# Complex mixing by three real products, and an inverse on half the rows of the array

## The chip, the cores and the metric

One core of one Trainium2 chip runs the kernel. The metric is the device time of one execution in microseconds (us), as the median of several runs. Three engines matter here besides the DMA queues: PE (TensorE, matrix products), DVE (VectorE) and ACT (ScalarE); POOL (GpSimd) and SP (SyncE) mainly issue DMAs. Each works through its own instructions in order and waits where an operand isn't there. Products write to PSUM, in eight banks; DVE and ACT read them out.

## The reference

```python
def _attn_ref(x, w_r, w_i, b_r, b_i):            # x: 2 x 3008 x 256
    X = np.fft.rfft(x, axis=1)
    Xr, Xi = X.real, X.imag
    Yr = Xr @ w_r - Xi @ w_i + b_r
    Yi = Xr @ w_i + Xi @ w_r + b_i
    Yr = np.sign(Yr) * np.maximum(np.abs(Yr) - 0.01, 0.0)
    Yi = np.sign(Yi) * np.maximum(np.abs(Yi) - 0.01, 0.0)
    return np.fft.irfft(Yr + 1j * Yi, n=3008, axis=1)

def _moe_ref(x, w_in, w_out):                    # 256 -> 2048 -> 256, on 6016 tokens
    h = x @ w_in
    return (h * np.clip(h + 3.0, 0.0, 6.0) / 6.0) @ w_out

def _moe2_ref(x, w_gate, w_val, w_out):          # 256 -> 1536 -> 256
    g = x @ w_gate
    return (g / (1.0 + np.exp(-g)) * (x @ w_val)) @ w_out
```

The output is the second of these on the first on the transform with its mixing. All is float32.

## The kernel before

The Fourier part is a transform in two stages (47 by 64) with tables, for two batches (`b`). The first stage (`pre`) writes through DRAM (`Bd`). Its 24 groups of frequencies are taken four at a time, so there are twelve **passes** `(b, Q)`, listed in `ORDER`. A pass has four kinds of work:

- `s2(b, Q, dh)`: the second stage, for either half `dh` of the 256 channels: four float32 products from `z` and the table `m` into one PSUM bank, which is then split into a rounded part `hi` and a remainder `lo` (float32r, tile `X`). Of the imaginary columns negated copies are kept too (`nhi`, `nlo`), so that a slice of 128 columns is either (re, im) or (-im, re).
- `ln(b, Q, h)`: the mixing with the weights, for two of the four groups (a "mixing half"). For each group, 12 products of 256 columns: two halves of the channels, two weights, and three products each for the split (`hi` by `wl`, `hi` by `wh`, `lo` by `wh`). The result has real parts on 64 rows and imaginary ones on the other 64. DVE then adds the bias (`yb`), clips to plus or minus 0.01 (`yc`) and subtracts (`yp`): that is the soft threshold.
- `ia(b, Q, h)`: the first stage of the inverse, two float32 products over 128 rows from `yp` and the table `n` (an "inverse half"); ACT copies them to `cs`, and the second half sends `cs` to DRAM (`Cd`).
- `conv1.step()`: a step of converting the first expert's weights, stored as 64-bit words, to float32r pairs, on ACT and DVE; `st` is loaded on SP.

The order of all this is written out by hand in `seq`. For pass p it is: first mixing half of p, first inverse half of p-1, the second stage of p+1 (two halves), second mixing half of p, second inverse half of p-1. From pass 8 on (`FROM`), four `unit()` calls of the first expert stand in between: a unit makes six products of 512 columns into `ph` for one block of 128 hidden features, gates the result (`r`: Relu on ACT, then a product with it on DVE), splits the tile of the unit before it (`lower`: rounded part on ACT, remainder on DVE), and makes six products of 512 columns of the unit two before into the accumulators. `later` holds an instruction back to the start of the next entry of `seq`. PSUM banks go round: eight until pass 7, then five (`few`), with three left to the accumulators.

After pass 7 `post` makes the first block of tokens from `Cd` (tile `ct`, by `inverse`). After the Fourier part the rest of the units run with preparations for the second scheme of the first expert (`plan`); there `fetch(0)` and `fetch(1)` load the first two weight slots, in units 11 and 13. All loads and most stores are issued on SP, in program order; the stores to `Cd` on POOL. The mixing weights are split by POOL in `split_lin`, ahead of the first pass.

Of the kernel before, what the change touches and what calls it, by code (L numbers as in the profile page):

```python
# [42 lines left out]
def dft_tables():  # L43
# [14 lines left out]
    for g in range(NG):  # L58
# [5 lines left out]
        for q in range(2):  # L64
# [3 lines left out]
            fwd2[g, q, 0, :, 0], fwd2[g, q, 0, :, 1] = c, -sn * sg  # L68
            inv1[g, 0, :, q, 0], inv1[g, 1, :, q, 0] = (w * c).T, -(w * sn * sg).T
            if g:  # L70
                fwd2[g, q, 1, :, 0], fwd2[g, q, 1, :, 1] = sn, c * sg
                inv1[g, 0, :, q, 1], inv1[g, 1, :, q, 1] = (w * sn).T, (w * ci * sg).T
    fwd2 = fwd2.reshape(NG, 128, 128).transpose(1, 0, 2).reshape(128, NG * 128)
    inv1 = inv1.reshape(NG, 128, 128).transpose(1, 0, 2).reshape(128, NG * 128)
# [9 lines left out]
def fourier_moe_kernel(ctx: ExitStack, tc: tile.TileContext, x, lin, bias, w1, w2, fwd1, inv2, fwd2,  # L84
# [52 lines left out]
    three = misc.tile([128, 64], F32, name="three")[:, :1]  # L137
    nc.vector.memset(three, 3.0)
    zeros = misc.tile([128, 512], F32, name="zeros")
# [79 lines left out]
    linh = ap_.tile([128, 2, 2, DIM], F32R, name="linh")  # L219
    linl = ap_.tile([128, 2, 2, DIM], F32R, name="linl")  # L220
    bias_sb = ap_.tile([128, DIM], F32, name="bias_sb")
# [37 lines left out]
    def prepare():  # L259
        lin_st = ap_.tile([128, 2, 2, DIM], F32, tag="z", name="lin_st", bufs=3)  # L260
        nc.gpsimd.dma_start(lin_st, lin)
        nc.gpsimd.dma_start(bias_sb, bias)
        for h in range(2):
            nc.gpsimd.memset(room[5][:, h * TC : (h + 1) * TC], 0.0)
        load_x(5)
        m_t[0] = table("m", fwd2, 0, "m0", 6)
        lins.append(lin_st)

    lins = []

    def split_lin():
        lin_st = lins[0]
        for dh in range(2):
            for k in range(2):
                hi, lo, st = linh[:, dh, k], linl[:, dh, k], lin_st[:, dh, k]
                nc.gpsimd.tensor_copy(hi, st)
                nc.gpsimd.tensor_tensor(out=lo, in0=st, in1=hi.bitcast(F32), op=ALU.subtract)
# [4 lines left out]
    def pre(n):  # L282
# [26 lines left out]
        if n in REFILL:  # L309
            load_x(REFILL[n])  # L310

# [22 lines left out]
    m_t, z_t, n_t, X, yp, cs = {}, {}, {}, {}, {}, {}  # L334
# [5 lines left out]

    def load_q(b, Q):
        if (b, Q) in z_t or Q >= NQ:
            return
        if Q not in m_t:
            m_t[Q] = table("m", fwd2, Q, f"m{Q}", 6)
# [6 lines left out]
    def s2(b, Q, dh):  # L352

        if dh == 0:
            t = ap_.tile([128, 2, 2, 4, 3 * K2], F32R, tag="X", name=f"X{b}_{Q}", bufs=2)
            X[b, Q] = [t[:, k] for k in range(2)]
        p = psf[0]([128, 4, 128], f"p2_{b}_{Q}_{dh}")
        for g in range(4):
            nc.tensor.matmul(p[:, g, :], z_t[b, Q][:, g, dh * 128 : (dh + 1) * 128], m_t[Q][:, g, :],
                             start=True, stop=True)  # L360
        hi, lo = (t[:, dh, :, K2:] for t in X[b, Q])
        nhi, nlo = (t[:, dh, :, :K2] for t in X[b, Q])
# [5 lines left out]
    later = []  # L368

    def run(f):  # L370
# [4 lines left out]
        f()  # L375

    def ln(b, Q, h):

        if Q not in n_t:
            n_t[Q] = table("n", inv1, Q, f"n{Q}", 6)  # L380
# [3 lines left out]
        xh, xl = X[b, Q]  # L384
        for i in range(2):
            g = 2 * h + i
            n = 0
            for dh in range(2):
                for k, at in ((0, K2), (1, 0)):
                    sl = (slice(None), dh, g, slice(at, at + 128))  # L390
                    wh, wl = linh[:, dh, k], linl[:, dh, k]
                    nc.tensor.matmul(p[:, i, :], xh[sl], wl, start=n == 0, stop=False)  # L392
                    nc.tensor.matmul(p[:, i, :], xh[sl], wh, start=False, stop=False)
                    nc.tensor.matmul(p[:, i, :], xl[sl], wh, start=False, stop=n == 3)  # L394
                    n += 1
# [751 lines left out]
```

## Time and profile before

| | us |
|---|---|
| runs | 1210.8, 1211.8, 1212.4; median 1211.8 |
| the profiled execution | 1209.68 |
| its span, first to last instruction | 1207.7 |
| PE busy | 1199.2 (99%) |
| DVE busy | 910.1 (75%) |
| ACT busy | 755.2 (63%) |
| Fourier part with its first 16 units, us of the span | 29 to 197 |

A busy share is the union of an engine's records. A product's record is longer than its place in the stream, since the next one starts while it runs out; so PE's pace is read from start to start. The granted clock of TensorE is 1.00 throughout.

### The profile page before, as it was taken

What the parts mean: (1) busy time and instruction counts of PE and PEld (TensorE: products, weight loads), DVE (VectorE), ACT (ScalarE), POOL (GpSimd) and SP (SyncE); (2) the same over time, 40 slices, a digit from 0 to 9 for tenths busy, and PEclk for the clock granted to TensorE, in tenths of its full rate; (3) what the DMA queues carried; (4) which work ended last, traced back from release to release, by engine and by line L of the source; (5) the groups of instructions that cost most, each with busy time, mean ns of one, the idle gap of its engine ahead of it and who ended that gap; (6) DMA issues with size and microseconds to landing.
All of it is one profiled execution on the core that took longest, in us unless ns stands there. A gap on an engine that the chain in (4) does not pass through costs nothing.

```text
span 1207.7 us, 16257 instructions
## 1 busy us (share of the span) xinstructions
PE 1199.2 (99%) x5794; PEld 1009.3 (84%) x5794; DVE 910.1 (75%) x1599; ACT 755.2 (63%) x1379; POOL 52.8 (4%) x81
## 2 busy tenths in 40 slices
PE   9999999999999999999999999999999999999998
PEld 3899888878888888888889888888888888888997
DVE  4577896798988988989988766766766766766665
ACT  2455565677777777777777555665665655655554
POOL 4000003500000000000000000000000000000000
PEclk9999999999999999999999999999999999999999
DMA  8966343764463554554453444644644644644551
GB/s 300 304 240 198 104 130 114 263 221 165 137 239 126 179 182 157 176 188 143 179 195 132 150 159 161 231 164 159 229 162 160 230 157 157 222 157 157 195 193 70
DMA packets 56720, 216.96 MB, mean 180 GB/s; under 512 B 5776, under 2 KB 17392, under 8 KB 44912
## 3 DMA queue, kind: packets, MB, share of 16 engines
q1 hardware_dynamic: 54000, 206.78, 48.6%
q0 software_dynamic: 2496, 9.05, 2.0%
q8 instruction: 45, 0.74, 0.2%
q14 instruction: 35, 0.29, 0.1%
q10 hardware_dynamic: 144, 0.11, 0.0%
HBM read 169.51 MB, written 46.40 MB: 179 GB/s over the span
## 4 chain that ended last, share of the span: by engine, by line
PE 93%; DVE 3%; DMA 2%; ACT 2%; issue 1%; SPq 0%; ACTq 0%; DVEq 0%
PE acc L125 12%; PE acc L127 12%; PE acc L126 11%; PE P L849 8%; PE P L851 8%; PE P L850 8%; PE Tb L849 4%; PE Tb L851 4%; PE Tb L850 4%; PE p L489 3%; PE Q L849 2%; PE Q L851 2%; PE Q L850 2%; PE p L297 2%; PE p L394 2%; PE p L392 2%
## 5 line engine op out<-in xcount | busy, mean ns | idle before, releaser
L905 ACT COPY hold<-P 128x512 f32<-128x512 f32 (+1 forms) x224 | 128.3, 573 | 78.0 <-PE P L851 77.9
L130 DVE TENSOR_TENSOR gated<-s,gated 128x512 fp32r<-128x512 f32 (+1 forms) x144 | 97.4, 676 | 49.8 <-ACT gated L1034 49.7
L527 ACT CAST gated<-r 128x512 fp32r<-128x512 f32 (+1 forms) x160 | 98.0, 613 | 54.8 <-DVE r L896 54.7
L900 DVE TENSOR_TENSOR hold<-Q,hold 128x512 f32<-128x512 f32 (+1 forms) x112 | 75.9, 678 | 64.9 <-PE Q L851 53.5
L125 PE MATMUL acc<-gated,w_o 128*128 128x512 f32 (+1 forms) x320 | 124.5, 389 | 0.0
L130 DVE TENSOR_TENSOR gated<-r,gated 128x512 fp32r<-128x512 f32 (+1 forms) x160 | 107.8, 674 | 21.9 <-ACT gated L527 18.2
L127 PE MATMUL acc<-gated,w_o 128*128 128x512 f32 (+1 forms) x320 | 123.2, 385 | 0.0
L126 PE MATMUL acc<-gated,w_o 128*128 128x512 f32 (+1 forms) x320 | 123.2, 385 | 0.0
L892 ACT ACTIVATE r<-hold,three 128x512 f32<-128x512 f32 (+1 forms) x120 | 85.7, 714 | 40.7 <-DVE hold L900 40.1
L127 PE MATMUL acc<-gated,slot 128*128 128x512 f32 (+1 forms) x288 | 111.1, 386 | 0.0
L125 PE MATMUL acc<-gated,slot 128*128 128x512 f32 (+1 forms) x288 | 111.0, 385 | 0.0
L126 PE MATMUL acc<-gated,slot 128*128 128x512 f32 (+1 forms) x288 | 110.9, 385 | 0.0
L900 DVE TENSOR_TENSOR hold<-P,hold 128x512 f32<-128x512 f32 (+1 forms) x112 | 75.8, 677 | 38.9 <-PE P L851 38.9
L1074 ACT ACTIVATE s<-hold 128x512 f32<-128x512 f32 (+1 forms) x72 | 44.9, 623 | 86.3 <-DVE hold L900 86.3
L900 DVE TENSOR_TENSOR hold<-Tb,hold 128x512 f32<-128x512 f32 (+1 forms) x112 | 76.0, 678 | 27.1 <-PE Tb L851 20.6
L849 PE MATMUL P<-xo,slot 128*128 128x512 f32 (+1 forms) x240 | 92.2, 384 | 2.5 <-DVE hold L900 1.2
L851 PE MATMUL P<-xo,slot 128*128 128x512 f32 (+1 forms) x240 | 91.6, 382 | 0.0
L896 DVE SCALAR_TENSOR_TENSOR r<-r,hold 128x512 f32<-128x512 f32 (+1 forms) x120 | 81.2, 677 | 13.7 <-ACT r L892 12.8
L850 PE MATMUL P<-xo,slot 128*128 128x512 f32 (+1 forms) x240 | 91.5, 381 | 0.0
L1034 ACT CAST gated<-s 128x512 fp32r<-128x512 f32 (+1 forms) x144 | 88.1, 612 | 1.9 <-DVE s L1089 1.9
L1079 ACT ACTIVATE s<-hold 128x512 f32<-128x512 f32 (+1 forms) x72 | 45.0, 625 | 50.4 <-DVE hold L900 50.4
L127 PEld LDWEIGHTS acc<-gated,w_o 128*128 128x128 f32 x320 | 60.1, 188 | 11.3
(174 smaller groups left out, 2919.8 us busy)
## 6 DMA issues: line engine op xcount, KB each, us to landing
slot<-Wd SPq DMA_DIRECT2D x72, 1152.0 KB, 5.1
slot<-Sd SPq DMA_DIRECT2D x40, 896.0 KB, 4.7
st<-in_w SPq DMA_DIRECT2D x68, 256.0 KB, 4.2
Wd<-slot SPq DMA_DIRECT2D x12, 1152.0 KB, 5.1
z<-Bd SPq DMA_DIRECT2D x12, 512.0 KB, 4.8
Cd<-cs POOLq DMA_DIRECT2D x12, 512.0 KB, 3.8
Xd<-x SPq DMA_DIRECT2D x20, 256.0 KB, 2.0
raw<-Xd SPq DMA_DIRECT2D x5, 1024.0 KB, 7.4
```

The source lines that it names most:

```text
L125: nc.tensor.matmul(o, wl, xh, start=start, stop=False)
L126: nc.tensor.matmul(o, wh, xh, start=False, stop=False)
L127: nc.tensor.matmul(o, wh, xl, start=False, stop=stop)
L130: nc.vector.tensor_tensor(out=o, in0=full, in1=hi.bitcast(F32), op=ALU.subtract)
L527: nc.scalar.copy(hi[:, :n], g[:, :n])
L849: nc.tensor.matmul(o, wl, x[m][:, 0, :n], start=start, stop=False, skip_group_check=not start)
L850: nc.tensor.matmul(o, wh, x[m][:, 1, :n], start=False, stop=False, skip_group_check=not start)
L851: nc.tensor.matmul(o, wh, x[m][:, 0, :n], start=False, stop=True, skip_group_check=not start)
L892: nc.scalar.activation(r[:, :n], x[:, :n], AF.Relu, bias=three)
L900: nc.vector.tensor_tensor(out=h, in0=x[:, :n], in1=c, op=ALU.add)
L905: nc.scalar.copy(c, x[:, :n])
L1034: nc.scalar.copy(hi[:, :nb], t[:, :nb])
```

## The change

- **Mixing.** `s2` no longer keeps negated copies. It writes three forms of a group of 64 columns: the real part, the imaginary part (the sign of the table is turned) and their difference, which is rounded and split as well (`both_`: a copy of 256 columns on ACT, a difference on DVE; `hi_s` on ACT and `lo_s` on DVE, held back by `later` and `last`). `ln` makes three real products, one for each form, each over both halves of the channels and with the split in three, so 18 products of 256 columns for two groups, where there were 24. Two go to one PSUM bank, the third to another. The result has two groups on the rows (64 each), real and imaginary parts in columns.
- **Bias.** It enters by a product: `ones` (64 rows, of which rows 0 and 32 are one) with `shift` (512 columns, rounded part in row 0 and remainder in row 32), into the first bank. `shift` holds bias plus 0.01.
- **Threshold.** ACT copies the third product (`k1`), DVE adds it to the other two (`yb`), ACT makes the Relu of `yb` - 0.02 (`yc`), and DVE adds min(`yb`, 0) to that (`yp`).
- **Inverse.** `ia` runs once a pass. Its contraction now lies over 64 rows and two products (real and imaginary part), so it makes eight float32 products on 64 rows, those of rows 0 to 63 into one bank and those of rows 64 to 127 into another, alternating.
- **Order.** In `seq` the inverse stands behind the second stage and ahead of the second mixing half.
- **Around it.** The tables `m` and `n` are loaded anew for the second batch, with three buffers for six. The mixing weights (three, with their difference and sum) and `shift` are split by DVE and ACT, in small steps behind `pre` 6 to 10 (`amid`); `split_lin` is gone, and POOL fills `ones`. `conv1.step()` runs in `ln` only for passes 1 to 7, and in units two times and once, in turn. `fetch(0)` and `fetch(1)` move to units 7 and 9.

The core of the diff:

```diff
-            fwd2[g, q, 0, :, 0], fwd2[g, q, 0, :, 1] = c, -sn * sg
+            fwd2[g, q, 0, :, 0], fwd2[g, q, 0, :, 1] = c, sn * sg
...
     def s2(b, Q, dh):
-            t = ap_.tile([128, 2, 2, 4, 3 * K2], F32R, tag="X", name=f"X{b}_{Q}", bufs=2)
+            t = ap_.tile([128, 2, 2, 3, 4 * K2], F32R, tag="X", name=f"X{b}_{Q}", bufs=2)
...
-        nc.scalar.copy(hi, p)
-        nc.scalar.mul(nhi, p[:, :, K2:], -1.0)
-        low(lo, p, hi)
-        later.append(lambda: nc.scalar.mul(nlo, X[b, Q][1][:, dh, :, 2 * K2 :].bitcast(F32), -1.0))
+        nc.scalar.copy(both_, p[:, 1])
+        nc.scalar.copy(hi, p)
+        nc.vector.tensor_tensor(out=both_, in0=p[:, 0], in1=both_, op=ALU.subtract)
+        low(lo, p, hi)
+        def then():
+            nc.scalar.copy(hi_s, both_)
+            last.append(lambda: low(lo_s, both_, hi_s))
+        later.append(then)
...
     def ln(b, Q, h):
-        if (b, Q) > (0, 0) and not conv1.done():
+        if 0 < ORDER.index((b, Q)) < FROM:
             conv1.step()
...
+        def product(o, form, k, start):
+            for dh in range(2):
+                xh, xl = (t[:, dh, form] for t in xs)
+                wh, wl = linh[:, k, dh], linl[:, k, dh]
+                nc.tensor.matmul(o, xh, wl, start=start and dh == 0, stop=False, skip_group_check=not start)
+                nc.tensor.matmul(o, xh, wh, start=False, stop=False, skip_group_check=not start)
+                nc.tensor.matmul(o, xl, wh, start=False, stop=dh == 1, skip_group_check=not start)
+        p = psf[0]([128, 2, DIM], f"p3_{b}_{Q}_{h}")
+        nc.tensor.matmul(p.rearrange("r c d -> r (c d)"), ones, shift, start=True, stop=True)
+        product(p[:, 1], 0, 0, False)
+        product(p[:, 0], 1, 1, False)
+        p1 = psf[0]([128, DIM], f"p4_{b}_{Q}_{h}")
+        product(p1, 2, 2, True)
+        nc.scalar.copy(k1, p1)
-        nc.vector.tensor_tensor(out=yb, in0=p, in1=bias_sb.unsqueeze(1).to_broadcast([128, 2, DIM]), op=ALU.add)
-        nc.vector.tensor_scalar(yc, yb, -LAM, LAM, op0=ALU.max, op1=ALU.min)
-        nc.vector.tensor_tensor(out=yp[b, Q, h], in0=yb, in1=yc, op=ALU.subtract)
+        nc.vector.tensor_tensor(out=yb, in0=p, in1=k1.unsqueeze(1).to_broadcast([128, 2, DIM]), op=ALU.add)
+        nc.scalar.activation(yc, yb, AF.Relu, bias=edges)
+        nc.vector.scalar_tensor_tensor(out=yp[b, Q, h], in0=yb, scalar=0.0, in1=yc, op0=ALU.min, op1=ALU.add)
+
+    def ia(b, Q):
+        p = [psf[0]([128, 2, DIM], f"p5_{b}_{Q}_{i}") for i in range(2)]
+        for h in range(2):
+            for c in range(2):
+                for i in range(2):
+                    r = slice(64 * i, 64 * i + 64)
+                    nc.tensor.matmul(p[i][:, h], n_t[b, Q][r, 2 * h + c, :], yp[b, Q, h][r, c, :], start=c == 0,
+                                     stop=c == 1, tile_position=(64 * i, 0))
...
-        seq += [l[0], a[0]] + u + some[:1] + S(p + 1)[:1] + u + S(p + 1)[1:] + [l[1]] + u + some[1:] + [a[1]] + u
+        seq += l[:1] + u + some + S(p + 1)[:1] + u + S(p + 1)[1:] + a + u + l[1:] + u
...
     def unit():
-        for _ in range(2):
-            if conv1.at < 2 * n + 6 and not conv1.done():
+        for _ in range(2 - n % 2):
+            if not conv1.done():
                 conv1.step()
...
-    plan(11, lambda: fetch(0))
-    plan(13, lambda: fetch(1))
+    plan(7, lambda: fetch(0))
+    plan(9, lambda: fetch(1))
```

## Rows read from the trace of the kernel before

**Rows 1.** The page's busy time, share of the span and instructions of each engine

```profile
PE 1199.2 (99%) x5794; PEld 1009.3 (84%) x5794; DVE 910.1 (75%) x1599; ACT 755.2 (63%) x1379; POOL 52.8 (4%) x81
```

**Rows 2.** PE timeline, one pass: start, length, line, out<-in, count, [idle before]

```profile
90.40 0.47 PE L392 MATMUL p<-linl,X 128*128 128x256 f32 x1
...
93.47 1.03 PE L408 MATMUL p<-yp,n 128*128 128x256 f32 x4
94.33 1.95 PE L359 MATMUL p<-m,z 128*128 128x128 f32 x16
96.03 0.36 PE L392 MATMUL p<-linl,X 128*128 128x256 f32 x1
...
98.99 1.03 PE L408 MATMUL p<-yp,n 128*128 128x256 f32 x4
99.67 0.47 PE L392 MATMUL p<-linl,X 128*128 128x256 f32 x1
```

**Rows 3.** PE timeline, a mixing half behind a product of 512 columns

```profile
129.66 0.39 PE L127 MATMUL acc<-gs,w_o 128*128 128x512 f32 x1
129.89 0.28 PE L392 MATMUL p<-linl,X 128*128 128x256 f32 x1
...
132.76 1.03 PE L408 MATMUL p<-yp,n 128*128 128x256 f32 x4
```

**Rows 4.** Stretches: length, busy us (instructions) by engine, clock, DMA share, GB/s

```profile
90.00:120.00 30.00, 29.71 (x223) 28.25 (x222) 22.73 (x50) 15.15 (x36) 2.26 (x3) 1.00 0.62 199
150.00:180.00 30.00, 30.00 (x188) 27.11 (x187) 28.02 (x69) 19.61 (x47) 0.75 (x1) 1.00 0.47 144
236.00:244.00 8.00, 7.36 (x32) 5.36 (x30) 7.30 (x12) 5.33 (x10) 0.00 (x0) 1.00 0.81 284
```

**Rows 5.** Groups by line until us 330: count, busy us, mean ns of one, idle before

```profile
L408 PEld LDWEIGHTS p<-yp,n 128*128 128x128 f32 x96 | 16.9, 189 | 1.8
```

**Rows 6.** DVE timeline: a conversion step, then the end of a mixing half

```profile
89.60 0.42 DVE L193 TENSOR_TENSOR w_o<-wt,w_o 128x256 fp32r<-128x256 f32 x1
89.93 0.29 DVE L173 TENSOR_SCALAR wt<-head 128x256 uint32<-128x256 uint32 x1
90.13 0.42 DVE L186 SCALAR_TENSOR_TENSOR wt<-head,wt 128x256 uint32<-128x256 uint32 x1
90.47 0.42 DVE L177 SCALAR_TENSOR_TENSOR wt<-st,wt 128x256 uint32<-128x256 uint32 x1
90.80 0.69 DVE L397 TENSOR_TENSOR yb<-p,bias_sb 128x512 f32<-128x512 f32 x1
91.52 0.43 DVE L399 TENSOR_SCALAR yc<-yb 128x512 f32<-128x512 f32 x1
91.98 0.69 DVE L401 TENSOR_TENSOR yp<-yb,yc 128x512 f32<-128x512 f32 x1
92.59 0.42 DVE L193 TENSOR_TENSOR w_c<-wt,w_c 128x256 fp32r<-128x256 f32 x1
```

**Rows 7.** Groups by line until us 330, of ACT

```profile
L892 ACT ACTIVATE r<-hold,three 128x512 f32<-128x512 f32 x24 | 17.4, 724 | 9.0 <-DVE hold L900 8.7
L364 ACT ACTIVATE X<-p 128x256 fp32r<-128x256 f32 x24 | 9.3, 389 | 0.0
```

**Rows 8.** PE timeline, the first mixing half and what follows it

```profile
32.39 0.68 PE L392 MATMUL p<-linl,X 128*128 128x256 f32 x1
...
36.17 0.50 PE L359 MATMUL p<-m,z 128*128 128x128 f32 x3
```

**Rows 9.** PE timeline, the first product with a fetched slot

```profile
244.48 0.47 PE L849 MATMUL P<-xo,slot 128*128 128x512 f32 x1 [1.12 <-DMA slot<-Sd]
```

**Rows 10.** PE timeline, the first token transform, after pass 7

```profile
109.58 2.84 PE L489 MATMUL p<-inv_sb,ct 96*128 96x94 f32 x24 [0.29 <-DMA ct<-Cd]
```

**Rows 11.** DVE timeline in the first stage

```profile
18.86 0.69 DVE L301 COPY first<-p 96x512 f32<-96x512 f32 x1 [1.03 <-PE p L297]
```

**Rows 12.** A group of DMA issues: count, KB each, us to landing

```profile
n<-in_inv SPq DMA_DIRECT2D x6, 256.0 KB, 6.1
```

More of the change, by code (lines that the diff above doesn't have):

```diff
@@ L265, in prepare, with mixed, hi, lo @@
         load_x(5)
[L266 to L277, printed above, removed]
+        load_m(0, 0)
+        o = spread("o_st")[:64, :128]
+        nc.gpsimd.memset(o, 0.0)
+        for r in (0, 32):
+            nc.gpsimd.memset(o[r : r + 1], 1.0)
+        nc.gpsimd.tensor_copy(ones, o)
+        w = [lin_st[:, k] for k in range(2)]
+        def mixed(op):
+            w.append(spread("mixed").rearrange("p (a b) -> p a b", b=DIM))
+            nc.vector.tensor_tensor(out=w[-1], in0=w[1], in1=w[0], op=op)
+        def hi(i, k):
+            nc.scalar.copy(linh[:, i], w[k])
+        def lo(i, k):
+            low(linl[:, i], w[k], linh[:, i])
+        def shifts(i):
+            b = b_st[:64]
+            if i == 0:
+                nc.vector.tensor_scalar(b, b, LAM, None, op0=ALU.add)
+                nc.scalar.copy(shift, b)
+            else:
+                low(shift[32:], b[32:], shift[32:])
+        amid.update({
+            6: [lambda: mixed(ALU.subtract), lambda: hi(2, 0)], 7: [lambda: mixed(ALU.add), lambda: hi(0, 2)],
+            8: [lambda: lo(2, 0), lambda: shifts(0)], 9: [lambda: lo(0, 2), lambda: hi(1, 3)],
+            10: [lambda: lo(1, 3), lambda: shifts(1)]})
+    amid = {}
+    def spread(name):
+        return xs_p.tile([128, 2 * DIM], F32, tag="r", name=name, bufs=3)
     first = w1p.tile([128, NT * TC], F32, tag="w1_o", name="first", bufs=1)
@@ L310, in pre @@
             load_x(REFILL[n])
+        for g in amid.pop(n, ()):
+            g()
     REFILL = {1: 6, 3: 7}
@@ L339, in table, with load_m @@
         return t
+    def load_m(b, Q):
+        if (b, Q) not in m_t:
+            m_t[b, Q] = table("m", fwd2, Q, f"m{b}_{Q}", 3)
     def load_q(b, Q):
@@ L343, in load_q @@
             return
-        if Q not in m_t:
-            m_t[Q] = table("m", fwd2, Q, f"m{Q}", 6)
+        load_m(b, Q)
         z_t[b, Q] = ap_.tile([128, 4, DIM], F32, tag="z", name=f"z{b}_{Q}", bufs=3)
@@ L375, in run @@
         f()
+        for g in last:
+            g()
+        last.clear()
     def ln(b, Q, h):
-        if Q not in n_t:
-            n_t[Q] = table("n", inv1, Q, f"n{Q}", 6)
-        if (b, Q) > (0, 0) and not conv1.done():
+        if (b, Q) not in n_t:
+            n_t[b, Q] = table("n", inv1, Q, f"n{b}_{Q}", 3)
+        if 0 < ORDER.index((b, Q)) < FROM:
             conv1.step()
-        p = psf[0]([128, 2, DIM], f"p3_{b}_{Q}_{h}")
-        xh, xl = X[b, Q]
-        for i in range(2):
[L386 to L395, printed above, removed]
@@ L403, in ia @@
[L403 to L411 removed]
+        xs = [t[:, :, :, h * 128 : (h + 1) * 128] for t in X[b, Q]]
@@ L1110 @@
     xp = np.pad(xp, ((0, 0), (0, QP - QN), (0, 0))).reshape(NB, QP, NJ // 8, 8 * DIM).transpose(0, 2, 1, 3)
-    bias = np.repeat(np.stack([b_r, b_i]), 64, axis=0)
+    bias = np.tile(np.concatenate([b_r, b_i]), (64, 1))
     def rows(w):
@@ L1128 @@
         "x": xp,
-        "lin": np.stack([rows(w_r), rows(w_i)], axis=2),
+        "lin": np.stack([rows(w_r), rows(w_i)], axis=1),
         "bias": bias,
```

56 lines of the change are left out of this document (29 added, 27 removed).

## The prediction, before the change was run

> **What bounds the kernel now.** I read the page's busy shares first, then the PE timeline, then DVE's, then the few places where PE waits. PE is busy 99% of the span [rows 1]; since the ends of matmuls are modelled, I check that by starts. In the stage that the change touches (us 29 to 197) the timeline of PE shows one pass after the other with nothing between: a pass takes 9.27 us, from 90.40 to 99.67, and consists of two mixing halves, the second stage and two inverse halves [rows 2]. A mixing half of 24 products takes 2.87 us (129.89 to 132.76), 0.12 us each; a product of 512 columns 0.23; an inverse half (four instructions) 0.86 (93.47 to 94.33) or 0.22 each; the second stage 1.70, or 0.106 for each of 16 [rows 2, 3]. So a product that PE no longer makes is time won, as long as the other engines keep up. DVE is the next: 22.7 of 30 us in the stage without units, 28.0 of 30 in a stretch with units [rows 4]. That margin is what this change spends.
>
> **PE, part by part.** *Three products:* each mixing half loses 6 of 24 products, 6 x 0.12 = 0.72 us, and gains one bias product of 512 columns, 0.23: -0.49, and over 24 halves -11.8 us [rows 3]. *Inverse on 64 rows:* twice as many instructions, 16 for 8 per pass, each streaming as long as now. If the two halves of the array run side by side, a pass has nine slots instead of eight (the two passes of one fp32 product use the same half, so a new partner starts one slot late): 9 x 0.213 = 1.92 for 1.71, +0.2 a pass, +2.5 in all. If they run one after the other it is 16 slots, 3.41, +1.7 a pass, +20.5 in all. *Going between 128 and 64 rows:* nothing in this trace uses 64 rows, so I bound it. The bias product too has 64 rows; where it follows an inverse, one change serves both. That makes 4 changes in a pass without units, 6 in one with units, 58 in all. Below, a change costs nothing; above, the next product waits until the one before is out (its record is 0.28 long against 0.12 from start to start, 0.16 more) and its weights are loaded, 0.19 [rows 3, 5]: 0.35. I take 0.1, since the nearest row is the change of number format, which costs 24 products 0.09 (2.96 behind the second stage, 96.03 to 98.99, for 2.87) [rows 2, 3]. PE alone: -11.8 + 2.5 + 5.8 = -3.5 us. The Trainium skill ("TensorEngine Tiling (Array Packing)", Key Properties) speaks against the change here: it says that changing the tiling mode drains TensorE. No run yet shows it; by it the switches would go to the upper bound, +20 instead of +5.8, which is a rival below. Of side-by-side running the skill ("TensorE: Matmul & The Clock Gate", Part 3) reports 3.07 times for four row tiles, which no row here shows either; by it nearer nine slots than sixteen.
>
> **What DVE and ACT gain in work.** Spacings of DVE from [rows 6]: 0.33 us for 256 columns, 0.61 for 512, 0.20 for a shift, 0.04 for a handover. *Second stage, each half:* DVE gets the sum and its low part, +0.66 to 1.27; ACT swaps two negations for two copies of the same size, about 0.4 each [rows 7]. *Mixing, each half:* ACT gets a copy of 256 columns (0.39) and the Relu of 512 (0.72) [rows 7]; DVE loses the clip (0.46), but yp now waits for ACT, and since DVE works in order all behind it waits too: 0.69 + 0.04 + 0.72 + 0.04 + 0.61 = 2.10, where now it is 0.72 + 0.46 + 0.61 = 1.79 [rows 6]. *Weight conversion:* 1.19 a step, two a pass [rows 6]. A pass on DVE now: 2 x 0.61 + 2 x 1.79 + 2.38 = 7.2 of 9.27. After: 2 x 1.27 + 2 x 2.10 + 2.38 = 9.1, with the waits for the first copies up to 9.5. PE's pass after: 2 x (0.23 + 18 x 0.12) + 1.70 + 1.92 + 0.4 = 8.8. **So DVE becomes the slower one**, by 0.3 to 0.7 a pass; PE runs on while buffers last (about 3 us), and pays later.
>
> **The sum, by stage**, with the three queues laid out in program order, each instruction starting when its engine and its operands are free (the walk; on the kernel before it gives 9.27 us a pass and no wait of PE after pass 0, as the trace has it). Pass 0: -1.5 (0.6 of PE work; and today's first half takes 3.78 us, 32.39 to 36.17, for 2.87, a wait of 0.9 that the bias and the first products now cover [rows 8]). Pass 1: +1.0: DVE has no slack left from pass 0, and the last six products wait 1.3 for the low part of the sum. Passes 2 to 7: -0.4 each for five, -0.1 for the one that ends on the token transform, -2.1; DVE falls behind by 0.6 a pass to 4.9 us. Pass 8: +1.8: from here five PSUM buffers go round, the inverse takes two at once, and the second is that of the first unit, which DVE reads only after its backlog (a wait of 2.0). Passes 9 and 10: after the first mixing half PE has 1.36 + 1.36 + 0.95 + 1.36 = 5.0 us until it needs the low half of the last unit's tile; DVE has 0.6 for the copy, 0.73 + 0.76 + 0.65 for the chain, two conversion steps 2.4, then 0.7: 5.9. So a wait of 0.9 against -0.2 of PE work, +0.7 each. Pass 11, which has no second stage to fill: wait 1.8, +1.6. The last unit and inverse: +0.4. Sum: -1.5 + 1.0 - 2.1 + 1.8 + 1.4 + 1.6 + 0.4 = +2.6.
>
> **Moved steps.** The two fetches go four units earlier; today PE waits 1.12 us for the slot at 244.48 [rows 9]. It lands early then, but DVE is busy 7.3 of 8 us there [rows 4] and comes next: -0.5 to -1.1, taken -1.1. The chain Cd store, ct load, token transform is tied to DVE and ACT, not to PE: PE waits 0.3 for it at 109.58 [rows 10] and, arriving 1.1 earlier, waits 1.4; DVE catches up meanwhile, so most comes back out of pass 8: +0.3. Splitting the weights moves from POOL to DVE and ACT, eleven instructions between copies before which DVE idles 1.03 of 1.72 us [rows 11]: nothing. Twelve more table loads on SP, of 256 KB, landing in about 6 us [rows 12], are asked for a pass (9 us) ahead: nothing; without that cover each costs PE its lateness, some 1 us. SP's waits for conversion buffers stand ahead of the z load; z is still due a pass later. The conversion goes from up to two steps a unit to three in two units: counted. **In all +2.6 + 0.3 - 1.1 = +1.8 us.** The profiled run took 1209.7 with a span of 1207.7; the median 1211.8 lies 2.1 above it. I add to the median: 1213.6.
>
> **Rivals.**
> *PE's saving comes through.* For it: DVE is at three quarters in the stage without units [rows 4], and the walk is sensitive: records of DVE and ACT 5% shorter take 3 to 4 us off. Against it: 9.1 us of DVE in program order is a floor unless yp's wait shrinks. PE alone then, with changes at 0 to 0.1: -9.3 to -3.5, and -1.1: 1201 to 1207, taken 1206.
> *The change of rows is dear.* 0.2 to 0.35 each instead of 0.1. By the drain that the Trainium skill states ("TensorEngine Tiling (Array Packing)", Key Properties) each change would lie there. For it: nothing can hide a weight load behind an array that has to run empty. Against it: format changes show only 0.09 [rows 2, 3]. PE's pass is then 9.2 to 9.9 and becomes the bound again; from 0.15 on the total is beyond 0.2%: 58 x 0.1 to 58 x 0.25 more, less what DVE's waits hide: +7 to +15, 1218 to 1227, taken 1220.
> *The halves don't run side by side.* Slower by one mechanism, in the inverse: sixteen slots in place of nine, 7 x 0.213 x 12 = +18 on PE; less some 2 us that DVE no longer delays, so +17 over the forecast, 1230. It decides from one slot more a pass, 12 x 0.213 = 2.6 us. Against it: the tables and yp are laid out so that partners use different rows and different PSUM buffers.
>
> **How the numbers follow.** Forecast 0.40 (its own range 1211 to 1217), saving comes through 0.30, dear changes 0.17, one after the other 0.13. About 0.2%, 2.4 us, is what can be told from no change. Faster: 0.30 and 0.02 of the forecast's case, 0.32. Same: 0.28 of the forecast's. Slower: its remaining 0.10, and 0.30: 0.40. The range 1204 to 1227 leaves out the best of the first rival and most of the last.
>
> **What would show it.** Right: in passes 2 to 7 halves of about 2.5 us and a pass of 8.9; DVE with nearly no idle there, and yp waiting for ACT; waits of PE for the low half of a gated tile in passes 9 to 11; no wait for the slot at the end. The inverse in about 1.9 us a pass with two starts close together (side by side), or 3.4 (not). Gaps around the bias product of over 0.2 us (dear). It is wrong if passes take 8.4 us or less, or over 9.3.

## The result, and the profile after

The changed kernel takes 1220.5 us in the median (1219.2 to 1221.0, four runs), the kernel before 1211.3 (1207.7 to 1212.4) beside it: a ratio of 1.0079, 95% interval 1.0056 to 1.0102. It is slower by 9.2 us where I had forecast 1.8. The profiled execution took 1220.05 us with a span of 1218.3, 10.6 more than before. The first line of the page after has the engines' busy time as [rows 1] have it before.

```profile
PE 1204.9 (99%) x5770; PEld 1000.6 (82%) x5770; DVE 919.0 (75%) x1631; ACT 777.4 (64%) x1431; POOL 49.7 (4%) x77
```

PE has 24 records fewer and 5.7 us more busy time. A busy time that grows while work is taken away means that something took longer, so I went to the timeline, pass by pass. This is PE's timeline after, from the second stage of one pass over the inverse and into the next pass (start, length, line, out<-in, count); [rows 2] answer to it.

```profile
83.84 1.95 PE L391 MATMUL p<-m,z 128*128 128x128 f32 x16
85.72 2.00 PE L459 MATMUL p<-yp,n 64*128 64x256 f32 x16
87.36 0.57 PE L438 MATMUL p<-shift,ones 64*128 64x512 f32 x1
87.86 0.39 PE L433 MATMUL p<-linl,X 128*128 128x256 f32 x1
...
90.00 0.28 PE L435 MATMUL p<-linh,X 128*128 128x256 f32 x1
90.21 0.49 PE L438 MATMUL p<-shift,ones 64*128 64x512 f32 x1
90.63 0.39 PE L433 MATMUL p<-linl,X 128*128 128x256 f32 x1
```

The inverse takes 1.64 us from its first start to the bias product (85.72 to 87.36), where eight slots of 0.21 make 1.7: the two halves of the array run side by side, without the ninth slot that I had counted. The bias product holds PE for 0.50 behind the inverse and 0.42 behind products on 128 rows, not 0.23. From one bias product behind an inverse to the next a pass takes 9.05 us (69.27, 78.31, 87.36 in the whole timeline), against 9.27 before and 8.8 in my sum. So up to here the change pays, by 0.2 us a pass.

DVE meanwhile falls behind. Its timeline after, one pass (the last column is the idle time ahead of an instruction and what ended it):

```profile
96.46 0.68 DVE L446 TENSOR_TENSOR yb<-p,k 128x512 f32<-128x512 f32 x1
97.93 0.69 DVE L450 SCALAR_TENSOR_TENSOR yp<-yb,yc 128x512 f32<-128x512 f32 x1 [0.79 <-ACT yc L448]
98.68 0.42 DVE L399 TENSOR_TENSOR sum<-p,sum 128x256 f32<-128x256 f32 x1
99.02 0.68 DVE L130 TENSOR_TENSOR X<-p,X 128x512 fp32r<-128x512 f32 x1
100.33 0.42 DVE L399 TENSOR_TENSOR sum<-p,sum 128x256 f32<-128x256 f32 x1 [0.64 <-ACT X L398]
100.68 0.68 DVE L130 TENSOR_TENSOR X<-p,X 128x512 fp32r<-128x512 f32 x1
...
106.44 0.68 DVE L446 TENSOR_TENSOR yb<-p,k 128x512 f32<-128x512 f32 x1
```

From `yb` to `yb` it is 9.98 us, with no gap but the waits in brackets: `yp` waits 0.79 for ACT twice a pass, as forecast, and `sum` waits 0.64 for ACT's `hi`, which I had not seen. DVE is the slower engine, by 0.9 a pass and not 0.3 to 0.7. Late `yp` means a late inverse, late `cs` copies on ACT, a late store to `Cd`, a late load of `ct`. The chain after (ACT, POOL, SP), and the same two issues of the kernel before:

```profile
101.10 1.07 ACT L462 COPY cs<-p 128x512 f32<-128x512 f32 x2
102.47 0.75 POOL L463 DMA_DIRECT2D Cd<-cs  x1 [9.22 <-ACT cs L462]
107.58 0.32 SPq L534 DMA_DIRECT2D ct<-Cd  x1
```

```profile
100.94 0.75 POOL L411 DMA_DIRECT2D Cd<-cs  x1 [8.51 <-ACT w_o L189]
104.25 0.32 SPq L482 DMA_DIRECT2D ct<-Cd  x1
```

The store goes out 1.53 us later, and the load, which waits for the store's landing, 3.33 later. So 1.8 of it is a store that lands later after its issue: 5.1 us from one issue to the other instead of 3.3 (the page has 4.7 us to landing for the twelve stores after and 3.8 before). The queue's packets show where the time goes: 2.8 us behind the issue all 144 packets of the store have moved in the kernel before, 136 of them in the changed one, and its last 8 (0.02 MB) trickle in until 4.4 us. Why they do is not tried. And then PE, after, at the first token transform (before: [rows 10]), with a table of stretches (length, busy us and instructions by engine, then the granted clock as a share, DMA share, GB/s):

```profile
112.35 5.32 PE L541 MATMUL p<-inv_sb,ct 96*128 96x94 f32 x24 [2.83 <-DMA ct<-Cd]
117.60 0.79 PE L438 MATMUL p<-shift,ones 64*128 64x512 f32 x1
```

```profile
109.00:112.00 3.00, 0.52 (x5) 0.31 (x3) 2.37 (x7) 2.39 (x6) 0.00 (x0) 0.96 0.88 254
112.00:114.00 2.00, 1.65 (x8) 1.68 (x9) 1.81 (x6) 1.20 (x5) 0.75 (x1) 0.50 1.05 392
114.00:117.00 3.00, 3.00 (x16) 3.00 (x16) 1.38 (x2) 1.16 (x2) 0.00 (x0) 0.50 1.07 409
117.00:120.00 3.00, 3.00 (x13) 2.48 (x13) 0.69 (x1) 0.58 (x1) 0.00 (x0) 0.50 0.31 120
120.00:122.00 2.00, 2.00 (x11) 2.00 (x11) 0.00 (x0) 0.00 (x0) 0.00 (x0) 0.50 0.00 0
122.00:124.00 2.00, 2.00 (x13) 1.74 (x13) 0.69 (x1) 0.84 (x2) 0.00 (x0) 0.99 0.00 0
```

PE waits 2.83 us, where I had forecast 1.4, and during the wait the clock falls from its upper level (2.4 GHz) to the lower (1.2 GHz): 0.50 for some 10.2 us (0.04 x 3 / 0.5 = 0.24 of the first stretch, ten whole ones, 0.04 of the last). PE has work for 9.7 us of that (112.35 to some 122.0), so half the clock costs about 4.8 us. The token transform takes 5.25 us to the next product where it takes 2.7 to 2.8 at full clock. No term of my sum stands for this. The Trainium skill ("TensorE: Matmul & The Clock Gate", Part 1, What's actually happening) says that "the default state is throttled, and activity releases the throttle"; the trace agrees in that the clock fell while PE waited and rose again while it worked.

Behind it the sums come out as forecast. From first mixing half to first mixing half, passes 9 and 10 take 0.75 and 0.6 us more than before, and from the one of pass 11 to the end of the last inverse it is 1.9 more. The wait for the low half of a gated tile is there, but shorter than I had it: in pass 9 the six products into the accumulators take 1.87 us where the others of their kind take 1.36, so PE waits 0.5 and not 0.9.

```profile
146.12 0.48 PE L125 MATMUL acc<-gs,w_o 128*128 128x512 f32 x1
...
147.99 1.05 PE L391 MATMUL p<-m,z 128*128 128x128 f32 x8
```

The wait for the fetched slot [rows 9] is gone: the first product with it follows without a gap.

```profile
254.40 0.39 PE L127 MATMUL acc<-gs,w_o 128*128 128x512 f32 x1
254.63 0.39 PE L901 MATMUL P<-xo,slot 128*128 128x512 f32 x1
```

Where the 10.6 us of span come from, by starts of PE after less before: -0.2 up to the start of pass 7; +3.0 to the start of the token transform, of which 2.5 is the longer wait; +2.6 the transform itself; +3.2 pass 8, of which some 2.2 is its first 4.4 us at half clock; +1.3 passes 9 and 10; +1.9 from pass 11 to the end of the inverse; -1.65 from there to the fetched slot; the rest, +0.5, is later.

### The profile page after: what moved, and what is told of

Its sections match the earlier page's. It is cut to its first block, busy times and chain, and to the rows that moved or that the text cites. A ratio compares the mean times of both kernels' runs of the same rounds, so it can differ in the third digit from the quotient of the medians.

```text
span 1218.3 us, 16275 instructions
## 1 busy us (share of the span) xinstructions
PE 1204.9 (99%) x5770; PEld 1000.6 (82%) x5770; DVE 919.0 (75%) x1631; ACT 777.4 (64%) x1431; POOL 49.7 (4%) x77
## 3 DMA queue, kind: packets, MB, share of 16 engines
q0 software_dynamic: 2496, 9.05, 2.2%
## 4 chain that ended last, share of the span: by engine, by line
PE 88%; DVE 5%; ACT 2%; DMA 2%; issue 2%; SPq 0%; POOL 0%; DVEq 0%; ACTq 0%; POOLq 0%
PE acc L127 11%; PE acc L125 11%; PE acc L126 11%; PE P L901 8%; PE P L903 8%; PE P L902 8%; PE Tb L902 4%; PE Tb L901 4%; PE Tb L903 4%; PE p L541 3%; PE Q L902 2%; PE Q L901 2%; PE Q L903 2%; PE p L459 1%; PE p L324 1%
## 5 line engine op out<-in xcount | busy, mean ns | idle before, releaser
L944 ACT ACTIVATE r<-hold,consts 128x512 f32<-128x512 f32 (+1 forms) x120 | 85.7, 714 | 40.9 <-DVE hold L952 40.0
```

Source lines behind the costliest of these rows:

```text
L944: nc.scalar.activation(r[:, :n], x[:, :n], AF.Relu, bias=three)
```

## Experiments

My theory, A: DVE's queue decides. It delays the chain to `ct`, PE's wait there drops the clock, and the two together are the loss. Rival B: the changes of rows are dear. Rival C: DVE's backlog has to be paid whatever the clock does, here or in a later pass. Unless another kernel is named, edits are made on the changed kernel and ratios are against the kernel before on the same chip, with a 95% interval.

### The clock kept up through the wait (e1_warm)

Three products with zeros, of 512 columns in float32, go into the bank that the token transform then overwrites.

```diff
         p = psf[0]([128, BLK], f"p6_{k[0]}_{eh}")
+        for _ in range(3 if k[0] == 0 and eh == 0 else 0):
+            nc.tensor.matmul(p, zeros[:, :128], zeros, start=True, stop=True)
         inverse(p, k, eh)
```

> Three products of 512 columns of zeros (float32, 0.85 us each) are added on PE just ahead of the first token transform; their result is overwritten by the transform. PE then has something to do in most of the 2.8 us in which it waits for ct. Theory A (the wait for ct and the clock that falls to half for 10.2 us after it make up most of the loss): the granted clock stays at 1.00, the token transform and the first mixing half of pass 8 run at full pace, ct still lands at about 112.3; 4 to 5 us less than the changed kernel, 1215 to 1216. Rival B (the loss is PE's own work, the changes between 128 and 64 rows): no change, or up to 0.5 us more. Rival C (DVE is behind, and PE just waits elsewhere if it doesn't lose time here): 0 to 2 us less, with longer waits in pass 8.

Measured: 1216.1 us, 1.0061 (1.0046 to 1.0076): 2 us less than the changed kernel by the ratios, 4 by the medians (the two were timed on different chips). By the ratios that is less than A's 4 to 5. PE's timeline and the stretches:

```profile
109.99 2.74 PE L551 MATMUL p<-zeros 128*128 128x512 f32 x6
113.11 2.84 PE L541 MATMUL p<-inv_sb,ct 96*128 96x94 f32 x24 [0.38 <-DMA ct<-Cd]
115.89 0.50 PE L438 MATMUL p<-shift,ones 64*128 64x512 f32 x1
```

```profile
112.00:115.00 3.00, 2.62 (x19) 1.92 (x18) 2.45 (x7) 2.20 (x6) 0.75 (x1) 1.00 1.04 359
115.00:118.00 3.00, 3.00 (x24) 2.70 (x24) 1.99 (x3) 1.26 (x3) 0.00 (x0) 1.00 1.06 395
```

The data come no earlier (the transform starts at 113.11), but with PE kept at work the clock stays at 1.00 and the transform takes 2.78 us. From the start of the transform to the fetched slot it is 137.9 us instead of 142.3, so 4.4 of the some 4.8 us that the half clock cost come back there, and 3.6 in all, since the transform starts 0.8 later. The clock alone is 2 to 4 of the 9 us; the wait itself and what lies behind it remain.

### 128 rows for the bias product (e2_rows128)

`ones` and `shift` get 128 rows, zero in the lower half. That spares two changes of rows a pass and leaves those around the inverse.

```diff
-    shift = ap_.tile([64, 2 * DIM], F32R, name="shift")
-    ones = ap_.tile([64, 128], F32R, name="ones")
+    shift = ap_.tile([128, 2 * DIM], F32R, name="shift")
+    ones = ap_.tile([128, 128], F32R, name="ones")
...
```

> The bias product takes 128 rows (64 more rows of zeros in both operands), so that 32 of the 58 changes between 128 and 64 rows go and the arithmetic stays. All theories: the bias product before a mixing half that doesn't follow the inverse goes from 0.42 to about 0.23 us. Rival B (changes of rows are the loss): 32 times 0.15 to 0.19, 5 to 6 us less. Theory A: PE only arrives earlier at the token transform and waits longer there, the clock still falls; a gain in passes 8 to 11 alone, 1 to 3 us less than the changed kernel, 1217.5 to 1219.5.

Measured: 1215.8 us, 1.0058 (1.0043 to 1.0073): by the ratios 2.5 to 3 us less than the changed kernel, as A has it. PE's timeline:

```profile
79.68 0.28 PE L436 MATMUL p<-linh,X 128*128 128x256 f32 x1
79.80 0.40 PE L439 MATMUL p<-shift,ones 128*128 128x512 f32 x1
80.03 0.28 PE L434 MATMUL p<-linl,X 128*128 128x256 f32 x1
```

The bias product now takes 0.23 to the next start, not 0.42, and the last product ahead of it 0.12, not 0.21. As long as DVE does not hold PE up a pass takes 8.7 us (59.93 to 68.61, from bias product to bias product) against 9.05: two changes are worth 0.35, or 0.17 each. That lies between my 0.1 and my bound of 0.35. Of B this much holds: some 58 x 0.07 = 4 us over my sum. The Trainium skill ("TensorEngine Tiling (Array Packing)", Key Properties) says that changing the mode drains TensorE; this trace agrees that a change costs time, 0.17 us and so half of what I had worked out for a drain; whether it is a drain it does not show. But PE comes earlier only to wait: from us 90 on it waits for DVE's `X`, and at the token transform it waits 2.56 us with the clock at half for 6.8 us.

### The threshold on DVE (e3_yc_dve)

DVE makes `yc` itself, so it no longer waits for ACT.

```diff
-        nc.scalar.activation(yc, yb, AF.Relu, bias=edges)
+        nc.vector.tensor_scalar(yc, yb, -2 * LAM, 0.0, op0=ALU.add, op1=ALU.max)
```

> yc is made on DVE (add, then max with 0) in place of the Relu on ACT, so that DVE no longer waits for ACT between yb and yp. yp then starts 0.5 us after yb ends instead of 0.8; a pass of DVE goes from 9.98 to about 9.4 us. Theory A (what makes ct late is DVE's backlog in passes 3 to 6): the copies to cs and so ct come 2 to 3 us earlier, PE's wait at the token transform is under 1 us, the clock stays up; 6 to 9 us less than the changed kernel, 1211 to 1214. Rival B (changes of rows): at most 1 us less. Rival C (ct is late because of the DMAs themselves): cs earlier, ct hardly, 0 to 2 us less.

Measured: 1210.7 us, 1.0014 (1.0004 to 1.0023): nearly all of the loss is gone. DVE's timeline around `yc`, and PE's at the transform (the bracket names ACT, but the start lies 4.85 us behind the issue of the load of `ct`, so the load is meant):

```profile
90.22 0.68 DVE L446 TENSOR_TENSOR yb<-p,k 128x512 f32<-128x512 f32 x1
90.93 0.43 DVE L448 TENSOR_SCALAR yc<-yb 128x512 f32<-128x512 f32 x1
91.40 0.69 DVE L450 SCALAR_TENSOR_TENSOR yp<-yb,yc 128x512 f32<-128x512 f32 x1
```

```profile
108.51 2.85 PE L541 MATMUL p<-inv_sb,ct 96*128 96x94 f32 x24 [1.11 <-ACT head L170]
```

DVE does more work and is done sooner: 0.43 us of its own stand in place of 0.79 of waiting, and the pass on DVE falls to 9.25 us (from `sum` at 85.75 to `sum` at 95.00). The load of `ct` goes out at 103.66 instead of 107.58, the clock stays at 1.00, and the fetched slot is reached at 245.28 instead of 254.63. This single line gives back 9.4 us up to that point and 8 by the ratios, as A has it; the changes of rows are all still there, so B is not the larger part. ACT is relieved of the Relu too; but ahead of its Relus it had stood waiting for DVE's `yb` (1.68 and 0.81 us in the pass shown of the changed kernel), so it is DVE's time that counts.

### The difference ahead of the copy (e4_sum_first)

```diff
-        nc.scalar.copy(hi, p)
         nc.vector.tensor_tensor(out=both_, in0=p[:, 0], in1=both_, op=ALU.subtract)
+        nc.scalar.copy(hi, p)
         low(lo, p, hi)
```

> In the second stage the difference stands ahead of the rounded copy hi in the program, so that DVE waits for the copy of 256 columns alone; in the changed kernel it starts only when hi is done (98.68 and 100.33, hi ends at 98.65 and 100.30). Theory A: the wait of 0.64 us before the second difference shrinks to under 0.2, a pass of DVE goes from 9.98 to about 9.4, and as with the Relu moved ct is earlier, the wait under 1 us, the clock stays up; 5 to 9 us less than the changed kernel. Rival B: at most 1 us less. If the order in the program is not what makes it wait: the same 0.64 and the same time.

Measured: 1219.9 us, 1.0093 (1.0072 to 1.0114): no gain, against my expectation. The timelines of DVE and of ACT:

```profile
101.02 0.42 DVE L398 TENSOR_TENSOR sum<-p,sum 128x256 f32<-128x256 f32 x1
102.08 0.69 DVE L130 TENSOR_TENSOR X<-p,X 128x512 fp32r<-128x512 f32 x1 [0.65 <-ACT X L399]
```

```profile
101.47 0.59 ACT L399 CAST X<-p 128x512 fp32r<-128x512 f32 x1 [0.83 <-DVE sum L398]
```

The order is only turned round: now ACT's read of the bank waits for the end of DVE's (101.02 + 0.42 = 101.44, then 101.47), and DVE waits 0.65 for ACT behind it. Both instructions only read `p`; they run one after the other all the same, in program order. The clock is at 0.50 for 6.8 us here, behind a wait of 2.60; but the one execution of the four with a mean clock of 1.000 took 1219.0 us all the same, so the clock is not the whole loss. The Trainium skill ("PSUM — Partial Sum Buffer", PSUM bank collisions raise a hardware error) says of the compiler back end that it puts a dependency between any two instructions of different engines on one bank, ACT and DVE and reads included; both traces agree. So in this kernel the wait is not to be ordered away while both engines read one bank.

### The inverse directly behind the first mixing half (e6_ia_early)

`yp` of the pass before is then needed earlier, and the chain to `ct` is shorter.

```diff
-        seq += l[:1] + u + some + S(p + 1)[:1] + u + S(p + 1)[1:] + a + u + l[1:] + u
+        seq += l[:1] + a + u + some + S(p + 1)[:1] + u + S(p + 1)[1:] + u + l[1:] + u
```

> The changed kernel with its inverse moved up in the order written by hand: directly behind the first mixing half, ahead of the second stage, so that its two copies to cs stand on ACT ahead of the second stage's copies, which wait for DVE. DVE's work and its 10 us a pass stay as they are. Theory A (the loss is the wait for ct, which comes from cs standing behind DVE's backlog, and the half clock after that wait): cs of pass 5 some 3 us earlier, no wait for ct over 1 us, the clock stays up; 5 to 7 us less than the changed kernel, although two more changes of rows a pass in passes 1 to 7 cost up to 0.4 us each. Rival C (DVE's backlog costs PE its time whatever the token transform does): PE waits elsewhere instead, in passes 6 to 8; 0 to 2 us less.

Measured: 1218.9 us, 1.0081 (1.0066 to 1.0096). The clock is at 1.00 and PE does not wait at the transform, yet the time is that of the changed kernel. PE's waits from us 30 to 105 (in all, times, longest), and one of them:

```profile
PE p L435 <- DVE X L130: 5.1, 6, 1.3
```

```profile
89.98 0.38 PE L435 MATMUL p<-linh,X 128*128 128x256 f32 x1 [1.32 <-DVE X L130]
```

A pass takes 10.5 to 11.0 us (bias products at 62.00, 72.48, 83.17, 94.20): the inverse had covered DVE's splitting of the second stage, and the mixing half now waits for it (5.1 us in all, against 1.3 in the changed kernel). Some 0.35 us a pass, 2.4 in the seven passes with an inverse before the transform, is an estimate from e2 for the two more changes of rows that this order needs. The rest is C: with DVE as loaded as here, what is saved at one place is paid at another. A, which had the clock and the wait as the whole loss, missed this run.

### Cures together (e8_rows_yc, e5_rows_yc_pool)

e8 has the edits of e2 and e3 together. e5 has, in addition, the remainder of the difference on POOL:

```diff
-            last.append(lambda: low(lo_s, both_, hi_s))
+            last.append(lambda: nc.gpsimd.tensor_tensor(out=lo_s, in0=both_, in1=hi_s.bitcast(F32), op=ALU.subtract))
```

> Two edits of before together: bias product on 128 rows, and yc on DVE. PE's pass should be 8.7 us or less, DVE's 9.25 as with yc on DVE alone. Theory A: DVE is the bound again in passes 3 to 7, so these gain little over yc alone (9.05 to 9.0 or so), and ct is late once more by 1 to 2 us; passes 8 to 11 gain 0.6 each; 1 to 3 us less than with yc on DVE alone if the clock stays up, 2 us more if it falls. Rival B (PE's changes of rows are the bound): 32 x 0.17, 5 us less than with yc on DVE alone.

> As the one with bias on 128 rows and yc on DVE, and the low half of the difference (lo_s, 256 columns, both operands in SBUF) on POOL, which is idle there: 0.66 us a pass off DVE, 8.6 us, under PE's 8.7. Theory A: now neither backlog nor late ct; passes of 8.7, the clock stays up; 3 to 5 us less than with yc on DVE alone, 0.2 to 0.4% less than the kernel before. If POOL's 0.7 us for each comes too late for the last six products of a mixing half: waits of PE there, no gain over yc alone.

Measured: e8 1211.8 us, 1.0016 (1.0002 to 1.0030), no better than e3; **e5 1205.2 us, 0.9961 (0.9945 to 0.9977), better than both kernels.** PE at the transform in e8; then, in e5, three bias products, one pass apart, and the transform:

```profile
108.00 4.63 PE L542 MATMUL p<-inv_sb,ct 96*128 96x94 f32 x24 [2.00 <-ACT cs L463]
```

```profile
60.59 0.40 PE L439 MATMUL p<-shift,ones 128*128 128x512 f32 x1
...
69.28 0.40 PE L439 MATMUL p<-shift,ones 128*128 128x512 f32 x1
...
77.97 0.40 PE L439 MATMUL p<-shift,ones 128*128 128x512 f32 x1
...
105.61 2.77 PE L542 MATMUL p<-inv_sb,ct 96*128 96x94 f32 x24
```

In e8 PE makes its passes in 8.7 us and then waits 2.0 for `ct`, with half the clock for 6.8 us: what the cheaper rows give is lost again. In e5 the load of `ct` goes out at 100.85 (e8: 103.33), PE does not wait there, the clock stays at 1.00, and the gain reaches the end. Passes 5 and 6 of e5 take 9.04 and 9.30 us instead of 8.69 (in pass 6 PE waits 0.34 for POOL's remainder), so PE also comes a little later to the transform than it might. Of the 2.5 us between the loads 1.4 is the earlier store (97.52 for 98.95), the rest the store's landing.

### More of DVE's work on POOL (e12_conv_pool)

On top of e5 the remainders of the weight conversion go to POOL too, and the store to `Cd`, which POOL issues, goes behind the remainder of the difference.

```diff
-            nc.vector.tensor_tensor(out=lo, in0=self.full.pop(i), in1=hi.bitcast(F32), op=ALU.subtract)
+            nc.gpsimd.tensor_tensor(out=lo, in0=self.full.pop(i), in1=hi.bitcast(F32), op=ALU.subtract)
```

> The kernel with bias on 128 rows, yc on DVE and lo_s on POOL, and two more edits for DVE: the low half of the weight conversion goes to POOL too, and POOL issues the Cd store behind lo_s rather than ahead of it. DVE's pass should fall from 9.3 to about 8.6 us, under PE's 8.7. Theory A (DVE is still what PE waits for there, 0.35 to 0.6 us in passes 4 to 6 and about 0.5 to 0.9 in passes 9 to 11): these waits go, 2 to 4 us less than without the two edits, 1200 to 1203. Rival C (POOL is late instead): waits for lo_s or for the low weights, no gain or a loss.

Measured: 1212.2 us, 1.0022 (1.0010 to 1.0034), worse than e5 and a miss for A. Passes 3 to 6 take 8.7 to 8.9 us, so DVE no longer bounds them. But `ct` is asked for at 103.35, 2.5 us later than in e5: 0.4 of it is the later store (97.94 for 97.52), 2.1 the store's landing. PE comes to the transform 0.6 us earlier than in e5 and waits:

```profile
107.78 3.10 PE L542 MATMUL p<-inv_sb,ct 96*128 96x94 f32 x24 [2.77 <-ACT head L170]
```

```profile
110.00:113.00 3.00, 3.00 (x16) 2.90 (x16) 1.57 (x3) 0.58 (x1) 0.00 (x0) 0.53 0.98 339
113.00:116.00 3.00, 3.00 (x19) 2.74 (x19) 0.86 (x2) 1.01 (x3) 0.54 (x1) 0.90 0.39 153
```

The bracket names ACT, which had long been done; the start lies 4.4 us behind the load's issue, as in the other kernels (4.3 in e11, 4.7 in e8, 4.8 in the changed kernel), so the load is meant. Ten executions of this kernel say what the clock is worth: nine with a mean granted clock of 0.995 to 0.998 took 1210.5 to 1213.1 us, and the one at 1.000 took 1206.7.

### The fetches alone (e7_before_fetch)

On the kernel before, the two fetches go four units earlier.

```diff
-    plan(11, lambda: fetch(0))
-    plan(13, lambda: fetch(1))
+    plan(7, lambda: fetch(0))
+    plan(9, lambda: fetch(1))
```

> The kernel before with only the two fetches moved, from units 11 and 13 to 7 and 9. The wait of 1.12 us for the slot goes. If nothing else is late there: 1.1 to 1.6 us less in the trace from unit 7 to the first products with the slot, and as much at the end. If DVE is next: half of it at most.

Measured once: 1208.2 us, with 1209.5 for the kernel before beside it. The wait of [rows 9] is gone, and from a unit right behind the Fourier part to that product it takes 38.9 us instead of 40.2, 1.3 less; I had put in 1.1. Of the execution as a whole one run can't tell 1 us.

### A late load of ct in the kernel before (e10_ct_mid, e11_ct_late)

If a wait for `ct` alone drops the clock, it should do so without the change. In pass 7 e10 issues the load after the first half of the second stage, e11 behind the second mixing half.

```diff
-        seq += [l[0], a[0]] + u + some[:1] + S(p + 1)[:1] + u + S(p + 1)[1:] + [l[1]] + u + some[1:] + [a[1]] + u
+        c = [lambda: load_ct(blocks[0])] if p == NQ + 1 else []
+        seq += [l[0], a[0]] + u + some[:1] + S(p + 1)[:1] + c + u + S(p + 1)[1:] + [l[1]] + u + some[1:] + [a[1]] + u
```

> The kernel before, with nothing changed but the place of one DMA issue: the load of ct goes from the end of pass 6 to after the first half of the second stage in pass 7, behind a weight load and a z load on SP. ct then lands about 1.3 us later, and PE waits about 1.7 us for it at the token transform where it waits 0.3 (row) to 0.5 now. Theory A: a wait this short leaves the clock up or makes it fall; if it stays up, 1 to 1.5 us slower than the kernel before; if it falls as in the changed kernel, 5 to 7 us slower. Rival B (the half clock has to do with the 64-row products, not with the wait): the clock stays up whatever the wait.

> As the last one, with the load of ct behind the second mixing half of pass 7 and so behind one more weight load on SP, which waits for its buffer: ct lands 5 to 6 us later than in the kernel before, and PE waits about 6 us. Theory A (an idle PE at this place is followed by half the clock): the granted clock falls to 0.50 for 7 to 10 us, which costs half of that: 9 to 11 us slower than the kernel before in all, with no 64-row product and no backlog of DVE in it. Rival B: the wait alone, 5 to 6 us slower, clock at 1.00.

Measured: e10 1214.0 us, 1.0029 (1.0018 to 1.0039); e11 1212.3, 1.0025 (1.0012 to 1.0037). The profiled execution of e10:

```profile
110.74 2.85 PE L490 MATMUL p<-inv_sb,ct 96*128 96x94 f32 x24 [1.58 <-DMA ct<-Cd]
```

The waits there are 1.58 and, in e11, 1.52 us, with the clock at 1.00. So the long wait that e11 was to make did not come: SP asked for `ct` at 105.87, as early as in e10 (106.00), and the run answers nothing on long waits. Nor was it the place in SP's order that set these times: in both SP came to the load before the store to `Cd` had landed and waited for that (4.9 and 2.8 us). The store landed so late, 5.2 and 5.6 us from its issue to the load's where the kernel before has 3.3, with loads of `z` and of weights, which the edit had put ahead of `ct`, running beside it; that these are the reason is not tried. But the profiled executions are the fastest of their kernels (1210.0 and 1209.4). In seven of the eight of e10 the mean granted clock is 0.996 to 0.998 and the time 1212.5 to 1214.7; in the profiled one it is 0.999. In e11 the four with 0.996 or 0.997 took 1213.1 to 1215.2, and of the six at 0.999 or 1.000 five took 1209.4 to 1211.4 and one 1213.95. Whether the wait in the slower ones was longer, or a wait of this length sometimes drops the clock and sometimes not, is not to be seen without their traces, and stays open. That loading `ct` later costs this kernel 3 to 4 us in the median, without any part of the change, is shown.

### The changed kernel once more (e13_after_again)

> The changed kernel once more, unchanged, on the chip and beside the runs of the others, so that its distance to them rests on one chip: 0.6 to 1.0% slower than the kernel before, the wait at the token transform and the half clock as before.

Measured: 1220.1 us, 1.0082 (1.0067 to 1.0098), on another chip.

```profile
114.01 5.32 PE L541 MATMUL p<-inv_sb,ct 96*128 96x94 f32 x24 [3.69 <-DMA ct<-Cd]
```

The wait is 3.69 us here, and the clock at 0.50 for 10.2 us again.

## Why the prediction was right and where it was wrong

**Right.** The time lies in the whole range, slower was the likeliest of the three outcomes, and much of the forecast's mechanism came: halves side by side, DVE as the slower engine, `yp` waiting 0.8 for ACT, a wait for `ct` at the token transform, and the gain of the fetches (-1.1; -1.65 here, -1.3 alone).

**Luck.** The size was off by 7 us. 1220.5 lies outside the forecast's own range, 1211 to 1217, and on the 1220 of the rival of dear changes, whose mechanism is only a part of it; that the whole range holds it is owed to the share that it gave the rivals. Passes 9 to 11 cost what I had given (+0.7 each, and +2.0 for pass 11 and the rest; measured +0.75, +0.6 and +1.9), but in passes 9 and 10 by two errors that cancel: the wait was 0.5 and not 0.9, and PE's own work came to 0.25 and 0.1 more than before where I had 0.2 less.

**The step that failed**, and that weighs most, is the sentence that gives the chain to `ct` +0.3: "DVE catches up meanwhile, so most comes back out of pass 8". I counted a wait of PE as time that others use. It was 2.83 us instead of 1.4, and behind it the clock was at half for 10.2 us. e1 shows that keeping PE at work through it gives back 2 to 4 us, and e3 that with an earlier `ct` the wait is down to 1.11 us and the half clock is gone. A part did come back, by an estimate: leaving out some 2.2 us for the clock, pass 8 cost 1.0 more than before, not 1.8. Of the miss, 2.3 us had come before that, in passes 0 to 6, as told below.

**Why the wait was twice as long.** Two terms. DVE's pass was 9.98 us, not 9.1 to 9.5: I let ACT and DVE read one PSUM bank at the same time, and they don't (0.64 a pass in the changed kernel; e4 turns it round and keeps it). And the store to `Cd` took 5.1 us from its issue to that of the load, 1.8 more than before; I had moved the chain as a whole and kept the landing of the trace of before. Between kernels it varies from 3.3 (e5) to 5.6 (e11); why is not tried.

**The price of a change of rows** was 0.17 us around the bias product, not 0.1: +4 over 58 changes. The inverse takes eight slots and not nine, so my guess that a partner starts a slot late put 0.28 a pass too much into the sum (1.92 for 1.64); the two errors about cancel. Yet the pass is 9.05 and not 8.8: its bare products make 2 x (0.23 + 2.15) + 1.70 + 1.64 = 8.1, so the four changes take some 0.95 where I had 0.4. That is 0.24 each, with the change of number format behind an inverse in it, which I had used as a row to go by and never as a term of its own. The same is hidden in my reading of [rows 2]: the second inverse half there takes 0.68 and not 0.86, and a mixing half behind an inverse half 3.07 and not 2.87. Passes 0 to 6 so gave -0.2 in all where I had -2.5: 1.1 of that is the pace of passes 2 to 6, 0.8 pass 0 (-0.7 for -1.5), and the first mixing half starts 0.5 later than before, which I did not follow up.

**The rivals.** *PE's saving comes through* fell in the changed kernel and is what e5 is: its condition, that the wait of `yp` goes, was named rightly, but the edit alone (e3) reached 1210.7, and with cheaper rows beside it (e8) no less; it took DVE's remainder on POOL as well. *The change of rows is dear* came at its lower edge: 0.17, where I let it decide from 0.15, and its sign was there, 0.28 us more around a bias product than on 128 rows. But passes were still 0.2 us shorter than before with it, and e3, with every change of rows in place, takes back nearly all of the loss. *One after the other* did not happen: 1.64 us for sixteen instructions. The causes do not add up: by the ratios it is -2 without the half clock, -8 with DVE relieved, -3 with cheaper rows, and the last two together give no more than the second alone, until `ct` too comes in time.

## What to carry to other kernels

When a change moves work to an engine that empties PSUM, lay out its queue with every wait in it, reads of one bank by two engines among them. It can be better to give that engine 0.43 us more of its own work than to let it wait 0.79 us for another. A wait of PE of 2 to 3 us is to be priced with what the clock does behind it, here 2 to 5 us more, so look first at the loads that PE meets with nothing else queued, and change their timing before PE's pace. Small products on half the rows cost more by the change than by their columns: filling them up with zeros to 128 rows took 0.35 us out of a pass in which PE did not wait.

## What the runs showed of the hardware

- The clock stayed at 0.50 well after PE had work again: 9.7 us in the changed kernel (112.35 to 122.0), though the products came back to back. In e2, e4 and e8 it was down for 6.8 us, in e12 for 3.4, with waits of 2.6, 2.6, 2.0 and 2.8: its length did not follow that of the wait. Nor did it always fall during the wait, as it did in the changed kernel: in e8 and e2 it fell 0.8 and 0.9 us after PE had begun to work again, in e4 and e12 2.4 us after.
- A change between 128 and 64 rows costs PE some 0.17 us, as half of the 0.35 that two of them around a bias product cost (e2). Sixteen products on 64 rows, in turns on the two halves, take the time of eight.
- ACT and DVE did not read one PSUM bank together: the second started 0.03 to 0.04 us after the first had ended, whichever came first in the program. Whether the chip asks for that or only the waits of these programs do, no run here tells.
- The token transform starts 4.3 to 5.4 us behind the issue of its load wherever PE waits for it; a store of 512 KB took 3.3 to 5.6 us until the load behind it was issued, and in the changed kernel the last 8 of its 144 packets account for that.
